# Key softmax on partitions, with bursts bound to places in TensorE's order, in an agent attention kernel with an MLP behind it

## The chip, the cores and the metric

The kernel runs on one core of one Trainium2 chip. The metric is the device time of one execution in microseconds. The core's engines are TensorE (PE in the profile; PEld is its weight load), VectorE (DVE), ScalarE (ACT), GpSimd (POOL) and SyncE (SP, which issues the DMAs). Each runs its own instructions in order.

## The reference

For four batches, 12480 tokens of 128 channels and 49 agents a batch:

```python
def sm(a, b):
    s = scale * (a @ b.transpose(0, 2, 1))
    s = s - s.max(-1, keepdims=True)
    e = np.exp(s)
    return e / (e.sum(-1, keepdims=True) + 1e-09)
a2k = sm(agents, k)
agent_v = a2k @ v
q2a = sm(q, agents)
x = (q2a @ agent_v).reshape(B * S, D)
h = x @ w_in            # 128 -> 2048
g = h - np.tanh(h)
return g @ w_out        # 2048 -> 128
```

The "key softmax" is `sm(agents, k) @ v`: each batch's 49 agents against all its keys.

## The kernel before, in words

Everything is built on a tile framework that places buffers, inserts semaphores and decides each engine's order by its own timeline; the program can add order edges, which wait for nothing by themselves but fix which instruction stands first in a queue (`hold`, L607; `issue_order`, L613).

The main loop (L791, in `fast`) runs over 100 blocks of 500 query columns, 8 steps a block; two blocks are a pair (16 positions, `pos`). A step is: m1 (L533), four matmuls of the queries' agent weights `pT` with the projected agent values in two parts (`awh`, `awl`), into a PSUM tile `h`; on ScalarE `y` = tanh (L548) and `z` = square (L550); on VectorE `g` = h*z (L553); on GpSimd `gh`, a rounded copy of g (L582); on VectorE `gl` = g - gh (L587); and m2 (L590), six matmuls (L600 to L602) that add to the block's output `acc`. m2 of a step is written two steps after its m1 (LAG1, LAG2). In every even block the last step is "plain": it has no gh and gl, and its m2 is L598. PSUM has three double banks for `h` and two banks, `misc`, for all else: the running `acc` holds one of them.

Beside the steps run jobs, written as generators: `start` takes the first stage of a job at the end of a step, and each later step takes one more stage, after its m1 and before its m2 (L808 to L814). Three kinds matter:

- `q_softmax` (L485) for the next pair, started at position QS = 3 from the second pair on. Its burst is 32 matmuls in 32-column tiles (L494): a quarter tile of q columns is stationary, the 49 agents move. Later stages reduce, copy (L502, L503), subtract on GpSimd (L505), take exp (L507), normalise and split.
- `q_transpose` (L520), which transposes its result (L525) and copies it to `pT` (L530), started at positions 13 and 2.
- The key softmax of the next batch, `phase1(b + 1)`: a list of 34 jobs, three to a pair, at positions KS = (4, 10, 15) for the first of them and VS = (5, 10, 13) for the rest: 13 score groups of 8 key tiles, the maximum, 13 value groups (`av`), the sum, and four projections.

In batches 1 to 3 a score group loads the agents, padded to 64 columns (`agz`), as the stationary operand and moves 128 keys: 8 matmuls into two halves of 64 partitions, so that agents lie on partitions and keys along the free axis (L279). ScalarE copies the result to `s` (L281), VectorE reduces each row to a maximum (L282). `max_in` (L284) joins the groups and the halves to one maximum for each agent, `mn`. A value group then has five stages: exp with that maximum as bias (L324, held behind the step's z); four transposes on TensorE, which bring keys back to partitions (L330); a ScalarE copy `ke` (L333); 8 matmuls of ke with 128 channels of v and a column of ones (L340); and an addition to `acc` in SBUF on VectorE (L352). Batch 0 is treated before the main loop with keys on partitions all the way: L300 and L311 bring its maximum to all partitions by a transpose and a ones matmul, L356 subtracts, L358 takes exp, L370 multiplies with v.

Of the kernel before, what the change touches and what calls it, by code (L numbers as in the profile page):

```python
# [12 lines left out]
F32 = mybir.dt.float32  # L13
# [4 lines left out]
ET = mybir.EngineType  # L18
# [47 lines left out]
QL = 0  # L66
QS = 3
T0 = 13
T1 = 2
KS = (4, 10, 15)  # L70
VS = (5, 10, 13)

# [25 lines left out]
class Build:  # L98
    def __init__(self, ctx, tc, aps):
        self.tc, self.nc = tc, tc.nc  # L100
        self.qT, self.kT, self.v, self.agT, self.wi, self.wo, self.outT = aps
        self.pool = lambda name, bufs=1, **kw: tc.tile_pool(name=name, bufs=bufs, **kw)
        self.const = ctx.enter_context(self.pool("const"))
        self.keep = ctx.enter_context(self.pool("keep"))
        self.small = ctx.enter_context(self.pool("small", 2))
        self.ph = ctx.enter_context(self.pool("ph", 3, space=PSUM))
        self.pmisc = ctx.enter_context(self.pool("pmisc", 2, space=PSUM))

    def begin(self, ctx, name):
# [8 lines left out]
    def constants(self):  # L118
        nc = self.nc
        c = self.const  # L120
        self.agz = c.tile([128, B, HALF], F32, tag="ag", name="ag")
        self.ag = self.agz[:, :, :A]
        nc.sync.dma_start(self.ag, self.agT.rearrange("b c a -> c b a"))
        nc.gpsimd.memset(self.agz[:, :, A:], 0.0)
        self.ident = c.tile([128, 128], F32, tag="ident", name="ident")
# [70 lines left out]
    def phase1(self, b):  # L196
# [36 lines left out]
        def scores(g):  # L233
            yield
            yield
            if g == 0:
                st["s"] = self.keep.tile([128, NG * 512], F32, tag="s", name="s", bufs=1)
                if b == 0:
                    st["mxp"] = self.work.tile([128, A, 2 * NG], F32, tag="mxp", name="mxp", bufs=1)
                else:  # L240
                    st["mxp"] = self.small.tile([128, NG], F32, tag="mxk", name="mxk")
                st["acc"] = self.small.tile([128, C + 1], F32, tag="acc", name="acc")
# [31 lines left out]
            ps = self.misc()  # L274
            w = n // 2 * 128
            for c in range(n // 2):
                for r in range(2):
                    to = ps[HALF * r : HALF * (r + 1), c * 128 : (c + 1) * 128]
                    nc.tensor.matmul(to, self.agz[:, b, :], kt[:, n // 2 * r + c, :], start=True, stop=True)  # L279
            yield  # L280
            nc.scalar.copy(st["s"][:, g * 512 : g * 512 + w], ps[:, :w])  # L281
            nc.vector.tensor_reduce(st["mxp"][:, g : g + 1], ps[:, :w], axis=AX.X, op=ALU.max)  # L282

        def max_in():  # L284
            yield
            yield
            if b:
                m = self.small.tile([128, 1], F32, tag="mk", name="mk")
                top = self.small.tile([128, 1], F32, tag="mt", name="mt")
                nc.vector.tensor_reduce(m, st["mxp"], axis=AX.X, op=ALU.max)  # L290
                nc.vector.tensor_copy(top[:HALF], m[HALF:])
                nc.vector.tensor_tensor(m[:HALF], m[:HALF], top[:HALF], ALU.max)
                nc.vector.tensor_copy(m[HALF:], m[:HALF])
                st["mb"] = self.small.tile([128, 1], F32, tag="mn", name="mn")
                nc.vector.tensor_scalar(st["mb"], m, -SCALE, None, ALU.mult)
                return
            m = self.small.tile([128, A], F32, tag="m", name="m")
            nc.vector.tensor_reduce(m, st["mxp"][:, :, 2 * EARLY :], axis=AX.X, op=ALU.max)
            ps = self.misc()
            nc.tensor.transpose(ps[:A, :128], m, self.ident)  # L300
# [16 lines left out]
        def av(g):  # L317
            vt = ahead("v", load_v, g, vb - 1) if b else None
            n = tiles(g)
            if b:  # L320
                w = n // 2 * 128
                e = st["s"][:, g * 512 : g * 512 + w]
                first = self.count()
                nc.scalar.activation(e, e, AF.Exp, bias=st["mb"], scale=SCALE)  # L324
                self.hold(first, self.act_at, (ET.Activation,))
                yield
                ps = self.misc()
                for c in range(n // 2):
                    sl = slice(c * 128, (c + 1) * 128)
                    nc.tensor.transpose(ps[:, sl], e[:, sl], self.ident)  # L330
                yield
                et = self.small.tile([128, 512], F32, tag="ke", name="ke")
                nc.scalar.copy(et[:, :w], ps[:, :w])  # L333
                yield
                ps = self.misc()
                for c in range(n // 2):
                    for r in range(2):
                        t = n // 2 * r + c
                        k = rows(g, t)
                        nc.tensor.matmul(  # L340
                            ps[HALF * r : HALF * (r + 1), : C + 1],
                            et[:k, c * 128 + HALF * r : c * 128 + HALF * (r + 1)],
                            vt[:k, t, : C + 1],
                            start=c == 0,
                            stop=c == n // 2 - 1,
                        )
                yield
                acc = st["acc"]
                if g == 0:
                    nc.vector.tensor_copy(acc, ps[:, : C + 1])  # L350
                else:
                    nc.vector.tensor_tensor(acc, acc, ps[:, : C + 1], ALU.add)  # L352
                return
            sv = st["s"][:, g * GT * A : (g * GT + n) * A].rearrange("p (t a) -> p t a", a=A)
            e3 = sv
            nc.vector.tensor_tensor(e3, sv, st["mb"][:, None, :].broadcast_to([128, n, A]), ALU.subtract)  # L356
            yield
            nc.scalar.activation(e3, e3, AF.Exp, scale=SCALE)  # L358
            yield
            vt = ahead("v", load_v, g, 1)  # L360
# [4 lines left out]
            flat = e3.rearrange("p t a -> p (t a)")  # L365
            for t in range(n):
# [31 lines left out]
        def sums():  # L398
            yield
            yield  # L400
            if b == 0:
# [15 lines left out]
                return  # L417
            acc = st["acc"]
            pt = self.misc()
            nc.tensor.matmul(pt[:, :A], acc[:, :C], self.sel, start=True, stop=True)  # L420
            rows_of = acc[:, C : C + 1].broadcast_to([128, 128])
            nc.tensor.matmul(pt[:, A:A2], rows_of, self.sel, start=True, stop=True)
            yield
# [61 lines left out]
    def q_softmax(self, halves, qt, res, TT=TT):  # L485
        nc = self.nc
        ps = self.misc()
        for t in range(GT):
            b, at, w = halves[t // BT]
            at += min(t % BT * TT, w - TT)  # L490
            for r in range(0, TT, QUART):
                m = min(QUART, TT - r)
                to = ps[r : r + m, t * A : (t + 1) * A]
                nc.tensor.matmul(to, qt[:, at + r : at + r + m], self.ag[:, b, :], start=True, stop=True)  # L494
        yield
        yield
# [83 lines left out]
    def high(self, g):  # L580
        gh = self.wtile("gh", NB["gh"])[:, : g.shape[1]].bitcast(F32R)
        self.nc.gpsimd.tensor_scalar(gh, g, 1.0, 0.0, ALU.mult, ALU.add)  # L582
        return gh

# [28 lines left out]
    def issue_order(self, engine, first):  # L613
        info = mybir.DependencyInfo(mybir.DependencyClass.NoSync, mybir.DependencyReason.DATA)
        last = None
        for i in list(self.nc.cur_bb.bb.instructions)[first:]:
            if i.engine == engine:
                if last is not None:
                    self.tc.add_manual_dep(i, last, info, reason="issue order")
                last = i.name  # L620

    def last_on(self, engine):
# [15 lines left out]
    def fast(self):  # L638
# [101 lines left out]
        run(rest0.pop(0))  # L740
        run(dec[0])
        live = []
        kq = []
# [18 lines left out]

        def foreground(n, i):
            h = self.m1(self.aw[blocks[n][0]], pT[n][0], i, width(n))
            while done:
                finish(done.pop(0))
            return h
# [13 lines left out]
        def out(keep):  # L781
            while len(r2) > keep:
                n, i, gh, gl = r2.pop(0)
                if i == 0:
                    acc[n] = self.misc()
                wf = self.wf[:, 2 * C * i :] if n == 0 else self.wo_f.rearrange("p c n -> p (c n)")
                self.m2(acc[n], i, gh, gl, wf)
                if i == HP - 1:
                    done.append(n)
# [56 lines left out]
        out(0)  # L846
        finish(done.pop(0))
        self.loads_first(early)

# [57 lines left out]
```

## Time and profile before

| | us |
|---|---|
| three runs | 2139.8, 2141.7, 2142.6 |
| median | 2141.74 |
| profiled execution | 2142.99 |
| its span | 2141.2 |
| granted TensorE clock | 0.996 |

The profile is of one execution. Busy times of TensorE overlap, since matmuls are pipelined: the start-to-start distance of two matmuls is what one of them takes of the engine. A matmul with f32 operands stands as two instructions ("x64" for 32 matmuls). In a row of groups, the numbers behind the bar are the busy time in us and the mean of one in ns, and behind the second bar the idle time just before. A row of the timeline gives start and duration in us; brackets hold idle time and what ended it.

### The profile page before, as it was taken

Reading aid. Unit: us, or ns where it says so; the run is one execution under the profiler, and the core shown is the slowest. Engines: PE = TensorE matmul, PEld = TensorE weight load, DVE = VectorE, ACT = ScalarE, POOL = GpSimd, SP = SyncE. Lnnn points to the kernel's source line nnn. Section 1 sums busy time; section 2 is a strip of 40 time slices with the busy share of each in tenths; the row PEclk is TensorE's granted clock in tenths of the full one; section 3 lists DMA queues with packets and bytes.
Section 4 is the critical chain, followed back from the end, with each engine's and each line's share of the span. In section 5 each row is a group of like instructions: output and inputs, shape, how many; then the busy total and the mean of one; then the engine's idle time right before and its main releaser. Section 6 shows DMA issues by size and latency. Waiting matters only on the chain.

```text
span 2141.2 us, 35133 instructions
## 1 busy us (share of the span) xinstructions
PE 2107.2 (98%) x13259; PEld 1658.2 (77%) x13259; DVE 1996.0 (93%) x2031; ACT 1820.5 (85%) x2136; POOL 1303.9 (61%) x858
## 2 busy tenths in 40 slices
PE   8999999999999999999999999999999999999998
PEld 7577778777777777777787777777777777778776
DVE  7899999889999998889999999988999999999998
ACT  3888888888888888888898888888888989899897
POOL 0366666556665556556576566655666767767666
PEclk9999999999999999999999999999999999999999
DMA  9312112110112111211001110111000000100000
GB/s 343 105 60 68 53 37 72 51 55 24 39 49 67 54 50 50 59 61 49 20 28 61 59 42 30 50 59 42 30 30 21 29 30 20 33 26 20 30 10 21
DMA packets 65345, 109.01 MB, mean 51 GB/s; under 512 B 3984, under 2 KB 44176, under 8 KB 65168
## 3 DMA queue, kind: packets, MB, share of 16 engines
q1 hardware_dynamic: 65168, 106.68, 15.2%
q8 instruction: 108, 1.77, 0.4%
q14 instruction: 69, 0.57, 0.1%
HBM read 81.10 MB, written 25.56 MB: 50 GB/s over the span
## 4 chain that ended last, share of the span: by engine, by line
PE 66%; DVE 18%; issue 6%; POOL 5%; ACT 4%; DMA 0%; POOLq 0%; SPq 0%; DVEq 0%; ACTq 0%
PE misc L602 12%; PE h L538 11%; PE misc L600 11%; PE h L539 11%; PE misc L601 10%; DVE g L553 9%; DVE gl L587 6%; POOL gh L582 4%; PE misc L598 3%; ACT y L548 2%; PE misc L340 2%; PE misc L494 2%; ACT z L550 1%; PE misc L279 1%; PE h L250 1%
## 5 line engine op out<-in xcount | busy, mean ns | idle before, releaser
L582 POOL TENSOR_SCALAR gh<-g 128x1000 fp32r<-128x1000 f32 (+1 forms) x743 | 1197.8, 1612 | 690.2 <-DVE g L553 387.5
L587 DVE TENSOR_TENSOR gl<-g,gh 128x1000 fp32r<-128x1000 f32 (+1 forms) x743 | 956.5, 1287 | 85.6 <-PE misc L602 42.9
L553 DVE TENSOR_TENSOR g<-h,z 128x1000 f32<-128x1000 f32 (+1 forms) x800 | 945.4, 1188 | 30.8 <-ACT z L550 28.8
L548 ACT ACTIVATE y<-h 128x1000 f32<-128x1000 f32 (+1 forms) x800 | 801.4, 1004 | 198.4 <-PE h L539 192.0
L550 ACT ACTIVATE z<-y 128x1000 f32<-128x1000 f32 (+1 forms) x800 | 823.1, 1041 | 29.2 <-DVE g L553 12.9
L538 PE MATMUL h<-pT,awh 98*128 98x500 f32 (+1 forms) x1600 | 662.5, 414 | 0.3
L539 PE MATMUL h<-pT,awl 98*128 98x500 f32 (+1 forms) x1600 | 622.0, 389 | 0.0
L602 PE MATMUL misc<-gl,wo_h 128*128 128x500 f32 (+1 forms) x1486 | 594.4, 400 | 8.2 <-DVE gl L587 7.9
L600 PE MATMUL misc<-gh,wo_l 128*128 128x500 f32 (+1 forms) x1486 | 581.7, 391 | 7.6 <-POOL gh L582 6.7
L601 PE MATMUL misc<-gh,wo_h 128*128 128x500 f32 (+1 forms) x1486 | 578.2, 389 | 0.0
L538 PEld LDWEIGHTS h<-pT,awh 98*128 98x128 f32 x1600 | 301.2, 188 | 79.8 <-issue 17.7
L539 PEld LDWEIGHTS h<-pT,awl 98*128 98x128 f32 x1600 | 303.3, 190 | 68.9 <-issue 14.5
L602 PEld LDWEIGHTS misc<-gl,wo_h 128*128 128x128 f32 x1486 | 279.0, 188 | 83.3 <-DVE gl L587 23.1
L600 PEld LDWEIGHTS misc<-gh,wo_l 128*128 128x128 f32 x1486 | 280.6, 189 | 75.3 <-POOL gh L582 21.6
L601 PEld LDWEIGHTS misc<-gh,wo_h 128*128 128x128 f32 x1486 | 279.7, 188 | 53.6
L505 POOL TENSOR_TENSOR qe<-qe,qm 126x392 f32<-126x392 f32 x50 | 46.9, 938 | 77.2 <-ACT qe L503 77.2
L517 POOL TENSOR_TENSOR pp<-qe,pp 126x392 fp32r<-126x392 f32 x50 | 55.6, 1113 | 59.6 <-ACT pp L515 59.5
L598 PE MATMUL misc<-g,wo_f 128*128 128x500 f32 (+1 forms) x196 | 90.0, 581 | 0.0
L758 ACT ACTIVATE o<-misc 128x500 f32<-128x500 f32 (+1 forms) x100 | 58.0, 580 | 16.2 <-PE misc L602 9.0
L530 ACT CAST pT<-misc 98x500 fp32r<-98x500 f32 (+1 forms) x100 | 56.7, 568 | 5.3 <-PE misc L525 4.4
L598 PEld LDWEIGHTS misc<-g,wo_f 128*128 128x128 f32 x196 | 36.9, 188 | 26.2 <-issue 22.5
L525 PEld LDWEIGHTS misc<-identr,pp 126*98 126x98 f32 x400 | 38.9, 127 | 18.4 <-POOL pp L517 6.5
(111 smaller groups left out, 853.7 us busy)
## 6 DMA issues: line engine op xcount, KB each, us to landing
kt<-kT SPq DMA_DIRECT2D x48, 512.0 KB, 3.7
qt<-qT SPq DMA_DIRECT2D x46, 500.0 KB, 3.5
outT<-o SPq DMA_DIRECT2D x46, 500.0 KB, 2.6
v<-v SPq DMA_DIRECT2D x36, 512.0 KB, 4.1
vt<-v SPq DMA_DIRECT2D x12, 512.0 KB, 5.8
raw<-w_in SPq DMA_DIRECT2D x4, 512.0 KB, 9.2
v<-w_out SPq DMA_DIRECT2D x4, 512.0 KB, 8.1
qt<-qT SPq DMA_DIRECT2D x4, 490.0 KB, 3.5
```

Of the source, the lines that this page charges most:

```text
L538: nc.tensor.matmul(h[:, c, :w], aw[0][:A2, sl], pT[:A2, :w], start=True, stop=False)
L539: nc.tensor.matmul(h[:, c, :w], aw[1][:A2, sl], pT[:A2, :w], start=False, stop=True)
L548: nc.scalar.activation(self.pair(y), h, AF.Tanh, scale=TSC)
L550: nc.scalar.activation(z, y, AF.Square)
L553: nc.vector.tensor_tensor(self.pair(g), h, self.pair(z), ALU.mult)
L582: self.nc.gpsimd.tensor_scalar(gh, g, 1.0, 0.0, ALU.mult, ALU.add)
L587: self.nc.vector.tensor_tensor(gl, g, gh.bitcast(F32), ALU.subtract)
L598: nc.tensor.matmul(acc[:, :w], wf[:, c * C : (c + 1) * C], gh[:, x], start=first, stop=last)
L600: nc.tensor.matmul(acc[:, :w], self.wo_l[:, f, :], gh[:, x], start=first, stop=False)
L601: nc.tensor.matmul(acc[:, :w], self.wo_h[:, f, :], gh[:, x], start=False, stop=False)
L602: nc.tensor.matmul(acc[:, :w], self.wo_h[:, f, :], gl[:, x], start=False, stop=last)
L758: nc.scalar.activation(o[:, at : at + w], acc[n][:, :w], AF.Copy, scale=GSC)
```

## The change

In batches 1 to 3 keys now lie on partitions. A score group is 32 matmuls in 32-column tiles, of the form of the query burst: a quarter key tile is stationary, the 49 agents move. Copy and reduction go over 392 elements instead of 512; partial maxima are kept per partition and agent, in a spare part of `s`, and `max_in` and `max_out` bring them to all partitions as for batch 0. A value group has four stages: the maximum is subtracted on GpSimd (held right behind the latest gh), exp is taken on ScalarE (held behind the latest z), e is the stationary operand of 8 matmuls (64 columns for even, 49 for odd tiles, in two column halves) with v moving, and VectorE adds 113 partitions to `acc`. The transposes and the copy `ke` are gone; so are the zero columns of `agz`.

In the main loop, each m1 and m2 group is noted in `stream`. The bursts of q, scores and values go through `burst`: their matmuls stand one behind the other, behind the last two noted groups, and the next six groups to be noted stand behind them. q_softmax starts one position sooner and has its burst a stage later, so that it stands after m1 of step 3 and not after m2; its copy and reduction come one step sooner. VS goes to (2, 7, 12).

```diff
-QS = 3
+QS = 2
-VS = (5, 10, 13)
+VS = (2, 7, 12)
...
 def scores(g):
-            w = n // 2 * 128
-            for c in range(n // 2):
-                for r in range(2):
-                    to = ps[HALF * r : HALF * (r + 1), c * 128 : (c + 1) * 128]
-                    nc.tensor.matmul(to, self.agz[:, b, :], kt[:, n // 2 * r + c, :], start=True, stop=True)
+            first = self.count()
+            for t in range(n):
+                for r in range(0, 128, QUART):
+                    to = ps[r : r + QUART, t * A : (t + 1) * A]
+                    nc.tensor.matmul(to, kt[:, t, r : r + QUART], self.ag[:, b, :], start=True, stop=True)
+            self.burst(first)
             yield
-            nc.scalar.copy(st["s"][:, g * 512 : g * 512 + w], ps[:, :w])
-            nc.vector.tensor_reduce(st["mxp"][:, g : g + 1], ps[:, :w], axis=AX.X, op=ALU.max)
+            nc.scalar.copy(st["s"][:, g * GT * A : (g * GT + n) * A], ps[:, : n * A])
+            nc.vector.tensor_reduce(st["mxp"][:, :, g], ps[:, : n * A].rearrange("p (t a) -> p a t", a=A), ...)
...
 def av(g):
+            first = self.count()
+            (nc.gpsimd if b else nc.vector).tensor_tensor(e3, sv, top, ALU.subtract)
+            if b:
+                self.hold(first, self.gh_at, (ET.Pool,))
+            yield
+            first = self.count()
             nc.scalar.activation(e3, e3, AF.Exp, scale=SCALE)
-            yield
+            if b:
+                self.hold(first, self.act_at, (ET.Activation,))
+            yield
+            if b:
+                ps = self.misc()
+                first = self.count()
+                for t in range(n):
+                    r = rows(g, t)
+                    odd = t % 2
+                    w = A if odd else HALF
+                    nc.tensor.matmul(
+                        ps[HALF * odd : HALF * odd + w, : C + 1],
+                        flat[:r, t * A : t * A + w],
+                        vt[:r, t, : C + 1],
+                        start=t < 2,
+                        stop=t >= n - 2,
+                    )
+                self.burst(first)
+                yield
...
-        jobs = [scores(g) for g in range(NG)] + [max_in(), max_out() if b == 0 else None, None]
+        jobs = [scores(g) for g in range(NG)] + [max_in(), max_out(), None]
...
 def q_softmax(self, halves, qt, res, TT=TT):
+        yield
         ps = self.misc()
+        first = self.count()
...
-        yield
+        self.burst(first)
         yield
...
+    def burst(self, first):
+        if self.stream is None:
+            return
+        names = [n for group in self.stream[-2:] for n in group]
+        for i in self.queued(first):
+            self.after(i, names)
+            names = [i.name]
+        self.gate = (len(self.stream), names)
+
+    def streamed(self, first):
+        at, names = self.gate
+        group = self.queued(first)
+        if len(self.stream) < at + 6:
+            for i in group:
+                self.after(i, names)
+        self.stream.append([i.name for i in group])
```

`queued` returns the TensorE instructions written since `first`; `after` adds order edges.

More of the change, by code (lines that the diff above doesn't have):

```diff
@@ L107, in __init__ @@
         self.pmisc = ctx.enter_context(self.pool("pmisc", 2, space=PSUM))
+        self.stream = None
     def begin(self, ctx, name):
@@ L240, in scores @@
                 else:
-                    st["mxp"] = self.small.tile([128, NG], F32, tag="mxk", name="mxk")
+                    st["mxp"] = st["s"][:, NG * GT * A :][:, : A * NG].rearrange("p (a g) -> p a g", g=NG)
                 st["acc"] = self.small.tile([128, C + 1], F32, tag="acc", name="acc")
@@ L286, in max_in @@
             yield
[L287 to L296, printed above, removed]
             m = self.small.tile([128, A], F32, tag="m", name="m")
-            nc.vector.tensor_reduce(m, st["mxp"][:, :, 2 * EARLY :], axis=AX.X, op=ALU.max)
+            part = st["mxp"] if b else st["mxp"][:, :, 2 * EARLY :]
+            nc.vector.tensor_reduce(m, part, axis=AX.X, op=ALU.max)
             ps = self.misc()
@@ L319, in av @@
             n = tiles(g)
[L320 to L325, printed above, removed]
-                yield
[L327 to L330, printed above, removed]
-                yield
[L332 to L353, printed above, removed]
@@ L620, in issue_order, with queued, after @@
                 last = i.name
+    def queued(self, first):
+        return [i for i in list(self.nc.cur_bb.bb.instructions)[first:] if i.engine == ET.PE]
+    def after(self, i, names):
+        info = mybir.DependencyInfo(mybir.DependencyClass.NoSync, mybir.DependencyReason.DATA)
+        for name in names:
+            self.tc.add_manual_dep(i, name, info, reason="order on TensorE")
+    def burst(self, first):
+        if self.stream is None:
+            return
+        names = [n for group in self.stream[-2:] for n in group]
[10 more added lines that the diff above has]
+        self.stream.append([i.name for i in group])
     def last_on(self, engine):
@@ L741, in fast @@
         run(dec[0])
+        self.stream, self.gate = [], (0, [])
         live = []
@@ L847, in fast @@
         finish(done.pop(0))
+        self.stream = None
         self.loads_first(early)
```

34 lines of the change are left out of this document (24 added, 10 removed).

## The prediction

> **What bounds the kernel now.** I read the page first, then the busy times of single stretches, then TensorE's timeline around the bursts that the change touches. A "pair" below is two blocks of 500 columns, sixteen steps of the main loop, so fifty pairs in all.
>
> ```profile
> span 2141.2 us, 35133 instructions
> PE 2107.2 (98%) x13259; PEld 1658.2 (77%) x13259; DVE 1996.0 (93%) x2031; ACT 1820.5 (85%) x2136; POOL 1303.9 (61%) x858
> PE 66%; DVE 18%; issue 6%; POOL 5%; ACT 4%; DMA 0%; POOLq 0%; SPq 0%; DVEq 0%; ACTq 0%
> ```
>
> TensorE is busy for 98% of the span and carries 66% of the chain that ended last, but VectorE is busy for 93% as well. A busy share of this size hides stages with different limits, so the next view takes three pairs apart: one in which three value groups (av jobs) are worked on, one with three score groups, and one late pair with no key work.
>
> ```profile
> core 0: us, PE busy (x) PEld busy (x) DVE busy (x) ACT busy (x) POOL busy (x), PEclk, DMA share, GB/s
> 357.20:400.50 43.30, 43.30 (x291) 34.46 (x290) 38.00 (x40) 37.98 (x45) 25.57 (x18) 1.00 0.20 61
> 650.90:693.20 42.30, 42.30 (x290) 32.76 (x288) 40.03 (x39) 35.70 (x42) 23.45 (x17) 1.00 0.20 63
> 1739.10:1778.20 39.10, 38.90 (x232) 30.89 (x231) 37.94 (x37) 34.73 (x40) 27.39 (x18) 1.00 0.08 27
> ```
>
> The reader is to see that an av pair takes 43.3 us and a score pair 42.3 us against 39.1 us without key work, and that in both TensorE never rests (43.30 of 43.30, 42.30 of 42.30) while VectorE, ScalarE and GpSimd have 2 us or more to spare. In those pairs only TensorE time counts. In the late pair VectorE has just 1.2 us left (37.94 of 39.10): there a delay to its chain shows. A batch's key work is 34 places in the job list (13 score groups, 3 for the maximum, 13 av groups, one sum, 4 projections), three to a pair, so over batches 1 to 3 there are about 13 score pairs, 13 av pairs, 8 mixed ones and 16 without.
>
> **TensorE's saving.** The bursts are costed from start to start, because the durations of pipelined matmuls overlap.
>
> ```profile
> 375.27 0.39 PE L600 MATMUL misc<-gh,wo_l 128*128 128x500 f32 x1
> 375.50 0.39 PE L601 MATMUL misc<-gh,wo_h 128*128 128x500 f32 x1
> 375.73 0.60 PE L330 MATMUL misc<-ident,s 128*128 128x128 f32 x4
> 376.08 0.47 PE L538 MATMUL h<-pT,awh 98*128 98x500 f32 x1
> 376.39 0.39 PE L539 MATMUL h<-pT,awl 98*128 98x500 f32 x1
> ...
> 381.40 0.49 PE L600 MATMUL misc<-gh,wo_l 128*128 128x500 f32 x1
> ...
> 681.00 0.39 PE L601 MATMUL misc<-gh,wo_h 128*128 128x500 f32 x1
> 681.32 1.09 PE L279 MATMUL misc<-kt,ag 128*64 128x128 f32 x16
> 682.35 0.49 PE L538 MATMUL h<-pT,awh 98*128 98x500 f32 x1
> 682.68 0.39 PE L539 MATMUL h<-pT,awl 98*128 98x500 f32 x1
> ...
> 1753.29 0.40 PE L601 MATMUL misc<-gh,wo_h 128*128 128x500 f32 x1
> 1753.62 0.90 PE L494 MATMUL misc<-ag,qt 128*32 128x49 f32 x64
> 1754.44 0.50 PE L602 MATMUL misc<-gl,wo_h 128*128 128x500 f32 x1
> 1754.78 0.39 PE L600 MATMUL misc<-gh,wo_l 128*128 128x500 f32 x1
> ```
>
> Stream matmuls follow each other every 0.23 us (375.27 to 375.50). The four transposes of an av group (L330) put 375.50 to 376.08 between two stream matmuls, 0.58 less 0.23, so 0.35 us, and the interval behind them is 0.31 instead of 0.23: 0.43 us in all. They vanish. The value burst itself (L340) keeps its number of passes, its 129 moving columns and its two column halves, with 49 instead of 64 stationary columns in the odd ones, and I leave it at 0.
>
> A score burst of today (L279, 16 passes) takes 1.35 less 0.23, and 0.10 behind it: 1.22 us. The new one has the form of the query burst (L494: 64 passes, 32 stationary columns, 49 moving), which costs 1.15 less 0.23, and 0.11: 1.03 us. That is 0.19 us less. Of the 39 groups 36 are full, and 36 x (0.43 + 0.19) is 22.3 us.
>
> The row for L494 has 64 passes in 0.82 us, 13 ns each, so passes into four column places do run beside each other. The Trainium skill, "TensorEngine Tiling (Array Packing)", Performance Considerations, speaks against this part: it says that a matmul has some 60 cycles of overhead and that no tiling factor should be taken from a dimension that is already small, and 49 columns lie below 60. By that page (an estimate from its figure, at the 2.4 GHz of "Trainium Kernel Development and Optimization", NeuronCore Architecture) the new burst would cost 64 x 25 ns / 4 = 0.40 us against some 0.43 for the old one, so no gain on scores and 7 us less in the sum; the measured rows, 0.82 and 1.03 from start to start, say that there is some, and they decide.
>
> New on TensorE is the maximum, which moves across partitions by a transpose and a ones matmul, as it does for batch 0 at the start:
>
> ```profile
> 32.14 0.29 PE misc L300
> 33.07 0.66 PE misc L311 x2
> ```
>
> That is 0.95 us for each of three batches, 3 us with what follows them. The net saving is 19 us.
>
> **The other engines.** These rows price what is removed and what comes.
>
> ```profile
> L324 ACT ACTIVATE s<-s,mn 128x512 f32<-128x512 f32 x36 | 25.5, 708 | 0.0
> L333 ACT COPY ke<-misc 128x512 f32<-128x512 f32 x36 | 21.1, 587 | 14.6 <-PE misc L330 14.6
> L281 ACT COPY s<-misc 128x512 f32<-128x512 f32 x36 | 21.1, 587 | 1.2 <-PE misc L279 1.0
> L503 ACT COPY qe<-misc 126x392 f32<-126x392 f32 x50 | 24.2, 483 | 17.7 <-DVE qm L502 17.7
> L507 ACT ACTIVATE qe<-qe 126x392 f32<-126x392 f32 x50 | 26.5, 529 | 0.0
> L505 POOL TENSOR_TENSOR qe<-qe,qm x50: 842/844/1785, 36.4 to 2070.7; 126x392 f32<-126x392 f32 x50
> ```
>
> ScalarE loses 0.71 + 0.59 + 0.59 and gets 0.48 + 0.53 us for each group, 0.87 less. VectorE keeps one reduction and one addition a group. GpSimd gets a subtraction of 128x392, 0.84 us like L505, 33 us in all on an engine that is 61% busy. None of this is worth time where TensorE has no rest; it is worth something only if a wait appears.
>
> **The new waits.** The change binds each q, k and e burst between two named groups of the stream: behind the last two groups written before it, ahead of the next six. TensorE works in order, so if the burst's input is late, m1 and m2 queue behind it. Today they fill such a wait. For scores the input is a key tile loaded two groups ahead, and a free misc bank, which I take as ready. For av it is a chain: GpSimd's gh of the step at which the job starts, then the subtraction, then exp, and two steps later the burst. Here is such a chain in an av pair:
>
> ```profile
> 381.96 0.39 PE L538 MATMUL h<-pT,awh 98*128 98x500 f32 x1
> 382.65 0.39 PE L539 MATMUL h<-pT,awl 98*128 98x500 f32 x1
> 382.88 0.40 PE L602 MATMUL misc<-gl,wo_h 128*128 128x500 f32 x1
> 383.08 1.01 ACT L548 ACTIVATE y<-h 128x1000 f32<-128x1000 f32 x1 [0.41 <-PE h L539]
> 384.12 1.04 ACT L550 ACTIVATE z<-y 128x1000 f32<-128x1000 f32 x1
> 385.19 1.20 DVE L553 TENSOR_TENSOR g<-h,z 128x1000 f32<-128x1000 f32 x1 [0.17 <-ACT z L550]
> 386.57 1.82 POOL L582 TENSOR_SCALAR gh<-g 128x1000 fp32r<-128x1000 f32 x1 [0.67 <-PE h L539]
> ```
>
> m1 ends at 383.04, gh at 388.39, 5.35 us later. With 0.84 and 0.53 and some 0.3 for three handovers (0.04 to 0.18 each in these rows), exp is done 7.0 us after m1, and up to one ScalarE operation (1.04) later if it finds the engine taken. Meanwhile TensorE has to run two more m1 groups (8 matmuls) and m2 up to one step back. At 381.40 to 382.88 it stood, at this m1, with two of six matmuls of the m2 four steps back done, so 4 + 18 of m2 are left: 30 matmuls of 0.227, 6.8 us. The binding itself keeps TensorE closer to the written order, where one group of four matmuls less is left: 26, 5.9 us. What else falls in the window decides:
>
> The job that starts at position 2 has the query burst (1.03) and a set of output transposes (about 0.3) ahead of it: 7.2 to 8.1 us against 7.0 to 8.0, a wait of 0 to 0.8, I take 0.2. At position 7 the step is the plain one, which has no gh; the subtraction goes behind the gh of step 6, ten matmuls or 2.3 us earlier, so 4.7 to 5.7 against 5.9: nothing. At position 12 only the transposes help: 6.2 to 7.1 against 7.0 to 8.0, a wait of 0 to 1.8, I take 0.4, near the end with the deeper order, since that is the one the trace shows. That is 0.6 us for an av pair, 8 us over 13, with bounds of 0 and 34. For the query and score bursts in all pairs I add 1 us, with the bounds in the rivals.
>
> **The sum.** 2143.0 us for the profiled execution (span 2141.2 and 1.8 around it), less 19, plus 9: 2133; the median of the runs before lies 1.2 lower, so 2132.
>
> **Rivals.** Everything ready: the bursts find their inputs, nothing waits, and the 19 us stay whole. For it speaks that the three positions are next to the query burst, on the plain step and next to the transposes; against it the narrow window at position 12. It gives 2123.
>
> The late exp: at positions 2 and 12 the chain has the length just worked out and TensorE the shorter window, with 0.8 and 1.8 us of idle TensorE in every av pair, 2.6 x 13 = 34 us, less 19 saved: 2157, slower than before. For it speaks that today's av burst has three steps between exp and its place and can be overtaken, and that the subtraction adds a handover on GpSimd. It decides from 0.5 us per av burst (19 us over 39). Against it: ScalarE is relieved by 0.87 us a group, and a TensorE that waits leaves the others less behind.
>
> The stream's own chain: a bound burst asks that the m2 three steps back be finished before the next m1 starts, four matmuls or 0.9 us sooner than today. In the 24 pairs without score or av jobs VectorE is 97% busy (37.94 of 39.10) and cannot deliver sooner; if TensorE waits 0.4 us behind the query burst in each, 10 us are gone and with 2142 the change is no change. What speaks for it is that late pair; against it that it is one place in sixteen steps.
>
> The tiling page's rule, as a mechanism here: passes below the fixed length gain nothing, the score part is 0 and 7 us are missing: 2139. The rows of L494 already show the price of this form, so it gets next to nothing.
>
> **Chances.** Forecast 0.38 (its own range 2126 to 2137), everything ready 0.10, cancelled 0.16, late exp 0.33, tiling rule 0.03. About 0.2%, 4.3 us, is what a measurement of this kernel can tell from no change. Faster is 0.48, from the first two; same 0.19, from the cancelled case and the tiling rule; slower 0.33. The range takes in the full saving with some 7 us below it, for gains that the start-to-start prices miss, and the late exp with 5 above: 2116 to 2162.
>
> **What would show it.** Right: L330 and L333 gone, score bursts of 64 passes with 0.82 us from their start to the next stream matmul, av pairs near 42.6 us and score pairs near 41.7, waits of TensorE for the exp line below 0.4 us on average, and the late pairs still at 39.1. Wrong: an average wait over 0.5 us ahead of the e matmuls; late pairs over 39.4; or VectorE, not TensorE, without rest in the av pairs, for which the subtraction beside gl would have to cost VectorE over 3 us a pair.

## The result

The changed kernel takes 2301.39 us (median of four runs, 2299.09 to 2302.46) against 2142.15 for the kernel before: a ratio of 1.0744, 95% interval 1.0726 to 1.0763. It is 159 us slower; 2132 was forecast, with a range up to 2162. Lines have moved: L532 and L533 are now m1, L595 to L597 m2, L488 the query burst, L278 the score burst, L337 the value burst with e stationary, L321 the subtraction on GpSimd, L326 exp.

The same page lines as before:

```profile
span 2300.6 us, 38536 instructions
PE 2144.3 (93%) x14885; PEld 1629.9 (71%) x14885; DVE 2034.3 (88%) x2028; ACT 1780.2 (77%) x2097; POOL 1297.0 (56%) x896
PE 54%; DVE 24%; ACT 9%; POOL 8%; issue 5%; DMA 0%; POOLq 0%; ACTq 0%; SPq 0%; DVEq 0%
```

TensorE fell from 98% to 93% busy and from 66% to 54% of the chain, and every other engine is busy for a smaller share of the longer span too: not a new bound, but waits. TensorE's idle time, the span less its busy time, rose from 34.0 to 156.3 us; these 122 us are most of the 159. The other 37 stand as busy time, at least in part because a matmul with another one right behind it counts for 0.23 us and one ahead of a stop for its whole 0.39. Three stretches show where. With pairs counted from 0 they are pairs 11 to 16 (projections and score groups of one batch), 17 to 22 (maximum and value groups) and 40 to 46 (no key work); first the kernel before, then the changed one; the columns are those of the prediction's table of pairs.

```profile
525.68:776.32 250.64, 249.06 (x1581) 194.53 (x1580) 239.97 (x234) 214.57 (x250) 151.25 (x103) 1.00 0.16 51
776.32:1033.60 257.28, 255.15 (x1636) 200.90 (x1635) 233.02 (x242) 222.68 (x263) 155.90 (x103) 1.00 0.16 50
1739.11:2012.34 273.23, 271.87 (x1611) 215.99 (x1610) 264.99 (x253) 242.70 (x274) 190.44 (x120) 1.00 0.08 27
```

```profile
571.53:833.07 261.54, 250.99 (x2171) 193.07 (x2169) 242.01 (x235) 211.10 (x249) 146.74 (x102) 1.00 0.16 49
833.07:1123.74 290.67, 263.13 (x1588) 193.87 (x1586) 245.22 (x240) 212.93 (x251) 163.44 (x116) 0.99 0.14 44
1883.14:2168.30 285.16, 275.13 (x1612) 215.30 (x1611) 260.51 (x253) 242.40 (x274) 183.47 (x120) 1.00 0.08 26
```

The score stretch lost 11 us, the value stretch 33 us, and even the seven late pairs lost 12 us, 1.7 each, although only their query burst was touched. In all three rows TensorE's own busy time is now well below the time of the stretch. What TensorE waited for, over the whole span (total in us, number of waits, longest in us):

```profile
PE misc L597 <- DVE gl L582: 67.8, 119, 1.5
PE misc L488 <- ACT pT L524: 27.6, 42, 0.9
PE misc L337 <- ACT s L326: 14.4, 14, 1.2
PE misc L595 <- POOL gh L576: 9.1, 19, 0.9
PE misc L337 <- ACT qe L497: 8.2, 12, 2.5
PE misc L519 <- ACT o L779: 7.8, 21, 0.7
```

Before, the first kind came to 7.9 us and the second and third did not occur. The second and the last belong together; this is TensorE in a late pair, and below it ScalarE:

```profile
1933.68 0.38 PE L597 MATMUL misc<-gl,wo_h 128*128 128x500 f32 x1
1934.45 0.48 PE L519 MATMUL misc<-identr,pp 126*98 126x126 f32 x4 [0.39 <-ACT o L779]
1935.59 0.90 PE L488 MATMUL misc<-ag,qt 128*32 128x49 f32 x64 [0.67 <-ACT pT L524]
1936.42 0.50 PE L595 MATMUL misc<-gh,wo_l 128*128 128x500 f32 x1
```

```profile
1933.83 0.56 ACT L779 ACTIVATE o<-misc 128x500 f32<-128x500 f32 x1
1934.96 0.57 ACT L524 CAST pT<-misc 98x500 fp32r<-98x500 f32 x1 [0.57 <-PE misc L519]
```

One misc bank goes from hand to hand: the output copy must leave it before the transposes can write, and pT must be copied out before the query burst can. The engines take turns, and TensorE, whose next stream groups may not pass the burst, stands for 0.39 and 0.67 us. The third kind, at the end of a value pair (TensorE, GpSimd, ScalarE):

```profile
1573.69 0.38 PE L597 MATMUL misc<-gl,wo_h 128*128 128x500 f32 x1
1575.28 1.09 PE L337 MATMUL misc<-v,s 128*64 128x129 f32 x16 [1.20 <-ACT s L326]
```

```profile
1571.93 1.82 POOL L576 TENSOR_SCALAR gh<-g 128x1000 fp32r<-128x1000 f32 x1 [0.39 <-PE misc L596]
1573.71 0.95 POOL L321 TENSOR_TENSOR s<-s,mb 128x392 f32<-128x392 f32 x1
```

```profile
1574.69 0.53 ACT L326 ACTIVATE s<-s 128x392 f32<-128x392 f32 x1 [0.53 <-POOL s L321]
```

gh ends at 1573.75, the subtraction at 1574.66, exp at 1575.22; TensorE was through with the groups ahead of the burst at about 1574 and waits for 1.2 us. The stop goes on behind it: no m1 starts between 1571 and 1577.7, and ScalarE gets no `h` for 3.72 us:

```profile
1578.94 1.93 ACT L542 ACTIVATE y<-h 128x1000 f32<-128x1000 f32 x2 [3.72 <-PE h L533]
```

### The profile page after: what moved, and what is told of

The parts are those of the page before. It is cut to its first block, busy times and chain, and to the rows that moved or that the text cites. A ratio compares the mean times of both kernels' runs of the same rounds, so it can differ in the third digit from the quotient of the medians.

```text
span 2300.6 us, 38536 instructions
## 1 busy us (share of the span) xinstructions
PE 2144.3 (93%) x14885; PEld 1629.9 (71%) x14885; DVE 2034.3 (88%) x2028; ACT 1780.2 (77%) x2097; POOL 1297.0 (56%) x896
## 4 chain that ended last, share of the span: by engine, by line
PE 54%; DVE 24%; ACT 9%; POOL 8%; issue 5%; DMA 0%; POOLq 0%; ACTq 0%; SPq 0%; DVEq 0%
DVE gl L582 11%; PE h L532 10%; DVE g L547 10%; PE h L533 9%; PE misc L597 9%; PE misc L595 8%; PE misc L596 8%; POOL gh L576 6%; PE misc L593 4%; ACT z L544 4%; ACT y L542 3%; POOL qe L499 1%; PE misc L337 1%; PE h L249 1%; PE misc L488 1%
## 5 line engine op out<-in xcount | busy, mean ns | idle before, releaser
L576 POOL TENSOR_SCALAR gh<-g 128x1000 fp32r<-128x1000 f32 (+1 forms) x743 | 1137.6, 1531 | 866.0 <-DVE g L547 758.2
L582 DVE TENSOR_TENSOR gl<-g,gh 128x1000 fp32r<-128x1000 f32 (+1 forms) x743 | 971.2, 1313 | 137.1 <-POOL gh L576 107.7
L542 ACT ACTIVATE y<-h 128x1000 f32<-128x1000 f32 (+1 forms) x800 | 791.4, 1002 | 167.4 <-PE h L533 163.1
L532 PE MATMUL h<-pT,awh 98*128 98x500 f32 (+1 forms) x1600 | 658.8, 412 | 2.9 <-DVE g L547 1.4
L597 PE MATMUL misc<-gl,wo_h 128*128 128x500 f32 (+1 forms) x1486 | 594.4, 403 | 67.8 <-DVE gl L582 67.8
L533 PE MATMUL h<-pT,awl 98*128 98x500 f32 (+1 forms) x1600 | 621.9, 389 | 0.0
L595 PE MATMUL misc<-gh,wo_l 128*128 128x500 f32 (+1 forms) x1486 | 595.6, 401 | 9.6 <-POOL gh L576 9.1
L597 PEld LDWEIGHTS misc<-gl,wo_h 128*128 128x128 f32 x1486 | 279.6, 188 | 176.2 <-DVE gl L582 122.8
L532 PEld LDWEIGHTS h<-pT,awh 98*128 98x128 f32 x1600 | 301.3, 188 | 104.9 <-issue 26.0
L533 PEld LDWEIGHTS h<-pT,awl 98*128 98x128 f32 x1600 | 303.0, 189 | 68.7 <-issue 13.7
L595 PEld LDWEIGHTS misc<-gh,wo_l 128*128 128x128 f32 x1486 | 280.5, 189 | 93.6 <-POOL gh L576 38.3
L499 POOL TENSOR_TENSOR qe<-qe,qm 126x392 f32<-126x392 f32 x50 | 70.9, 1418 | 52.9 <-ACT qe L497 52.9
L497 ACT COPY qe<-misc 126x392 f32<-126x392 f32 x50 | 24.3, 485 | 87.2 <-DVE qm L496 87.2
L511 POOL TENSOR_TENSOR pp<-qe,pp 126x392 fp32r<-126x392 f32 x50 | 49.2, 983 | 74.4 <-ACT pp L509 74.4
L488 PE MATMUL misc<-ag,qt 128*32 128x49 f32 (+1 forms) x3200 | 45.6, 210 | 27.9 <-ACT pT L524 27.6
```

The costliest lines, as they stand in the source:

```text
L499: nc.gpsimd.tensor_tensor(ev, ev, m[:TT, :, None].broadcast_to([TT, GT, A]), ALU.subtract)
L532: nc.tensor.matmul(h[:, c, :w], aw[0][:A2, sl], pT[:A2, :w], start=True, stop=False)
L533: nc.tensor.matmul(h[:, c, :w], aw[1][:A2, sl], pT[:A2, :w], start=False, stop=True)
L542: nc.scalar.activation(self.pair(y), h, AF.Tanh, scale=TSC)
L582: self.nc.vector.tensor_tensor(gl, g, gh.bitcast(F32), ALU.subtract)
L595: nc.tensor.matmul(acc[:, :w], self.wo_l[:, f, :], gh[:, x], start=first, stop=False)
```

## The experiments

The theory: all of the loss comes from binding the bursts, by way of inputs that are late while nothing may pass. Rivals: the new key softmax itself costs it; or the forced order of m1 and m2 does. "Value pairs" and "score pairs" in the expectations are means over pairs 7, 8, 19, 20, 32, 33 and over 3, 14, 15, 26, 27, 28. In kernels without binding, work moves over a pair's edge, so the stretches above, in us, are the better measure:

| kernel | whole | score | value | late |
|---|---|---|---|---|
| before | 2142.2 | 250.6 | 257.3 | 273.2 |
| changed | 2301.4 | 261.5 | 290.7 | 285.2 |
| e1 nothing bound | 2140.0 | 252.8 | 252.3 | 273.2 |
| e2 query burst free | 2260.6 | 254.2 | 291.4 | 273.1 |
| e3 transposes later | 2277.6 | 259.5 | 293.6 | 273.2 |
| e4 before, query burst bound | 2210.2 | 264.5 | 259.2 | 285.4 |
| e5 value bursts free | 2224.4 | 262.8 | 265.2 | 285.2 |
| e6 following groups may pass | 2141.5 | 253.4 | 253.8 | 273.1 |
| e7 one group looser | 2288.3 | 259.0 | 290.7 | 285.2 |
| e8 score bursts alone bound, looser | 2161.6 | 260.8 | 253.8 | 273.2 |
| e9 value burst a step later | 2209.8 | 262.1 | 259.5 | 285.2 |
| e10 nothing bound, score bursts whole | 2119.6 | 245.6 | 253.2 | 273.1 |
| e11 e9 and e3 | 2201.3 | 260.0 | 268.7 | 273.0 |
| e12 e11 and e7 | 2206.4 | 261.8 | 268.0 | 273.1 |

e1, e8 and e10 were timed four to ten times, with the kernel before beside them; each of the others is one execution. Thirteen executions of the kernel before lie between 2139.5 and 2143.1 us, so differences of a few us between single ones mean little. In e2 and e3 the granted clock over the span was 0.985 and 0.989, against 0.995 in the changed kernel; e2 shows what lies behind that.

**e1, nothing bound.**

```diff
-        self.stream, self.gate = [], (0, [])
+        self.stream, self.gate = None, (0, [])
```

> The changed kernel with no burst bound to a place: keys on partitions, the new positions and the subtraction on GpSimd stay. Theory 1, the binding costs the time (TensorE stands at bursts whose bank or whose exp is not ready): all of the 159 us go, and the 19 us of TensorE work saved show, 2120 to 2140 us, late pairs (no key work) back at 39.1 us. Rival, the key softmax itself costs it (the subtraction and the handover on GpSimd delay gh and gl): value pairs stay above 48 us, and the time above 2220 us.

2139.95 us, ratio 0.9992 (0.9982 to 1.0002): the loss is gone, so the key softmax with keys on partitions doesn't cost it. The saving, though, is not there: the value stretch is 5 us shorter than before, the score stretch 2 us longer. The timeline of TensorE shows one score burst in four pieces:

```profile
1195.62 0.39 PE L533 MATMUL h<-pT,awl 98*128 98x500 f32 x1
1195.94 0.46 PE L278 MATMUL misc<-ag,kt 128*32 128x49 f32 x22
1196.33 0.50 PE L595 MATMUL misc<-gh,wo_l 128*128 128x500 f32 x1
1196.67 0.39 PE L596 MATMUL misc<-gh,wo_h 128*128 128x500 f32 x1
...
1197.58 0.38 PE L533 MATMUL h<-pT,awl 98*128 98x500 f32 x1
1197.89 0.38 PE L278 MATMUL misc<-ag,kt 128*32 128x49 f32 x16
1198.20 0.49 PE L597 MATMUL misc<-gl,wo_h 128*128 128x500 f32 x1
...
1199.44 0.39 PE L596 MATMUL misc<-gh,wo_h 128*128 128x500 f32 x1
1199.76 0.46 PE L278 MATMUL misc<-ag,kt 128*32 128x49 f32 x22
1200.15 0.49 PE L597 MATMUL misc<-gl,wo_h 128*128 128x500 f32 x1
...
1200.94 0.39 PE L597 MATMUL misc<-gl,wo_h 128*128 128x500 f32 x1
1201.26 0.28 PE L278 MATMUL misc<-ag,kt 128*32 128x49 f32 x4
1201.47 0.50 PE L595 MATMUL misc<-gh,wo_l 128*128 128x500 f32 x1
```

Start to start, less 0.23 each, the pieces take 0.48, 0.39, 0.48 and 0.30, and every one has an interval of about 0.34 instead of 0.23 behind it: 2.1 us for a burst that, reckoned so, costs 1.02 whole (e10, below: 1.15 less 0.23, and 0.33 behind it). Only 11 of the 36 full bursts ran whole.

**e2, query burst free.** `self.burst(first)` is taken out of q_softmax; score and value bursts stay bound.

> The changed kernel with only the query burst free again, score and value bursts bound. Theory 1: the query burst waits in every pair for the misc bank, which goes from the output copy to the transposes, from them to the copy of pT, and only then to the burst. The late pairs, which have no other bound burst, fall from 40.7 to 39.1 us, and some 1.7 us in each of 46 pairs go: about 2222 us. Rival, the late pairs are slower for another reason than the bound query burst: they stay at 40.7 and the time near 2300.

The late pairs are back at 39.0, as expected, and the score stretch loses 7 of its 11 us. But the whole is 2260.6, 39 us above the expectation: in the value stretch nothing is won. There the bound value burst now waits for the bank that the free, later query burst holds:

```profile
PE misc L337 <- ACT qe L496: 44.0, 12, 3.7
```

Each of these 12 waits ends within 1.0 us of the start of a stretch of 3.4 or 6.8 us in which TensorE's clock is granted at one half (the 0.50 in the first row); the stream's matmuls then stand 0.42 us apart instead of 0.23:

```profile
934.60:941.40 6.80, 6.03 (x26) 4.92 (x27) 3.04 (x7) 1.54 (x3) 2.39 (x3) 0.50 0.27 78
938.28 0.62 PE L596 MATMUL misc<-gl,wo_h 128*128 128x500 f32 x1
938.70 0.62 PE L594 MATMUL misc<-gh,wo_l 128*128 128x500 f32 x1
```

Leaving out the first 60 and the last 30 us, e2 has 13 such stretches, in which half the clock adds up to 27 us; the changed kernel has three, with 5 us, and e1 and the kernel before have none. So up to 22 of the 39 us can be the clock, a second price of a long wait.

**e3, transposes later.**

```diff
-T1 = 2
+T1 = 5
```

> The changed kernel with the transposes of the pair's second block started at position 5 and not 2, so that they no longer stand ahead of the bound query burst in the misc bank; all bursts stay bound. Theory 1a, the bank chain: the late pairs fall to 39.1 to 39.5 us and the whole to 2215 to 2240. Theory 1b, the binding costs by the order that it forces on m1 and m2 and not by the bank: the late pairs stay above 40.3 and the time above 2285.

The late pairs are back at 39.0 with the query burst still bound, so there it was the bank and not the order of the stream. The whole fell by 24 us only, to a time between the two theories' ranges: the value stretch got 3 us longer, since its burst waits longer for the query's copy (29.0 us over the span, 8.2 in the changed kernel), and the half clock takes 8.5 us in it where it took 1.7.

**e4, the kernel before with the query burst bound.** QS = 2, the burst at step 3, `burst` and `streamed` as in the change; the key softmax untouched.

> The kernel before with the query burst alone treated as in the change (bound, started at position 2, burst at step 3); its key softmax with agents on partitions is untouched and its bursts free. Theory 1: some 1.7 us in every pair, late pairs at 40.7 us and the whole at 2205 to 2230 us. Rival, the key softmax itself costs the time: 2142 within 5 us.

2210.2, as expected: late pairs 40.8, and 14 us more in the score stretch. Binding costs the old key softmax as well.

**e5, value bursts free.** `self.burst(first)` is taken out of av.

> The changed kernel with only the value bursts (e stationary) free again; query and score bursts stay bound. Theory 2, binding the value bursts is what costs in the value pairs: they fall from 51.0 us to the 41.4 of the kernel without any binding plus the 1.7 of the bound query burst, about 43.1, and the whole to 2190 to 2210 us. Rival, in the value pairs too the query burst and its bank are the cause: they stay above 47 and the whole above 2245.

77 us of the 159 go, 25 of them in this one value stretch. The whole misses its range by 14 us, and value pairs stand at 44.4 for 43.1: the query burst costs more in them than the 1.7 of a late pair.

**e7, one group looser.**

```diff
-        names = [n for group in self.stream[-2:] for n in group]
+        names = [n for group in self.stream[-1:] + self.stream[-4:-3] for n in group]
```

> The changed kernel with all bursts bound, but one group looser: behind the last m1 and behind the m2 before the last one, so that the m2 of three steps back need not be finished first; the next six groups still stand behind the burst. Theory 2a, most of the loss comes from the forced order of m1 and m2 (VectorE's gl is not there yet): waits of TensorE for gl in the value pairs fall from 2.8 us to under 1, value pairs to 45 to 47, the whole to 2215 to 2245. Theory 2b, most comes from bursts whose own input is late and which nothing may pass: value pairs stay above 49, the whole above 2270.

The whole is 2288.3, and value pairs stay at 50.5 with the same waits for gl: theory 2b there, bursts whose own input is late. For the score bursts this run is no clean test: an m2 may now pass into a burst, and only 12 of the 36 full ones ran whole, where all 36 did in the changed kernel. The score stretch gains 2.5 us all the same.

**e9, value burst a step later.** One more `yield` between exp and the burst, all bursts bound.

> The changed kernel with one more step between exp and the value burst, all bursts bound. If late exp is what counts (the rival of the prediction that ended on the slower side): the 1.2 us of waiting for exp in a value pair go, with the waits that follow from them, value pairs at 47 us or less and the whole at 2250 or less. If it is the forced order of the stream: value pairs lose those 1.2 us at most, 49.5 to 51, the whole 2280 to 2300.

2209.8, the first case: the value stretch falls by 31 of its 33 us. TensorE's waits, first kinds:

```profile
PE misc L598 <- DVE gl L583: 39.7, 90, 1.5
PE misc L489 <- ACT pT L525: 18.6, 32, 0.9
```

The 14.4 us of waiting for exp and the 8.2 for the query's copy are gone, and 28 us of the waits for gl with them, so those came with the stops at the value bursts. How they come about is argued, not shown: while TensorE stands at the burst it runs no m1, and the chain from m1 to gl, 7 us long, starts late. In the trace of the changed kernel the waits for gl stand 8 to 16 us behind the bursts that waited for the query's copy, and none stands within 16 us behind a wait of 1.2 us for exp. Nor does e9 say which of the two waits costs how much: the burst asks for its bank a step later as well, so it takes both away.

**e8, score bursts alone bound, in the looser form.**

> The changed kernel with only the score bursts bound, in the looser form, query and value bursts free. Without any binding 25 of 36 score bursts are cut into two to four pieces and score pairs take 43.0 us against 42.1 before; a whole burst saves the 0.2 us that each further piece costs. If the pieces are the reason: score pairs at 41.5 to 42.2, the whole at 2122 to 2132 us, faster than both kernels. If a bound score burst costs by the order it forces, as query and value bursts do: score pairs above 43 and the whole 2140 or more.

2161.64, ratio 1.0096 (1.0079 to 1.0113): slower than the kernel before, and the hoped-for case did not come. Twelve score bursts now wait for the bank with the free query burst's result, 17.2 us:

```profile
PE misc L278 <- ACT qe L495: 17.2, 12, 2.0
```

Nor were the bursts whole: in the looser form 22 of the 36 full ones were cut. So this run does not answer whether the pieces cost the time; e10 does.

**e10, nothing bound, score bursts whole.** To e1, each matmul of a score burst gets an order edge to the one ahead of it, and from the second on they are written under `tc.high_priority()`.

> The changed kernel without any binding, but with each score burst kept whole: its matmuls stand one behind the other, and from the second on they go ahead of everything else in the program's order; where the burst begins is left free. Without binding 25 of 36 full score bursts were cut into two or more pieces, and score pairs took 43.0 us. If the pieces cost that time: score pairs at 41.3 to 42.0 us, value and late pairs as without binding (41.4 and 39.0), the whole at 2118 to 2130 us, which would be the saving of 19 us that the prediction worked out. If pieces are cheap and something else slows the score pairs: still 42.7 to 43.3, the whole 2136 to 2144.

2119.58, ratio 0.9899 (0.9882 to 0.9915), against 2141.04 of the kernel before: 1.0% faster than before, and the fastest here. The same stretches:

```profile
521.32:766.95 245.63, 245.11 (x2170) 194.74 (x2169) 236.70 (x235) 211.15 (x250) 152.41 (x102) 1.00 0.17 53
766.95:1020.15 253.20, 250.76 (x1587) 195.66 (x1586) 240.77 (x240) 212.76 (x250) 178.63 (x116) 1.00 0.17 51
1716.37:1989.49 273.12, 271.73 (x1611) 216.02 (x1610) 264.97 (x253) 242.65 (x274) 190.79 (x120) 1.00 0.08 27
```

And TensorE at one of its score bursts:

```profile
674.71 0.38 PE L600 MATMUL misc<-gl,wo_h 128*128 128x500 f32 x1
675.02 0.90 PE L281 MATMUL misc<-ag,kt 128*32 128x49 f32 x64
675.86 0.50 PE L598 MATMUL misc<-gh,wo_l 128*128 128x500 f32 x1
676.19 0.39 PE L599 MATMUL misc<-gh,wo_h 128*128 128x500 f32 x1
```

The burst has 0.84 us to the next start, and in this stretch TensorE is busy for 245.11 of 245.63 us again. The 21.5 us saved are close to the net 19 that the prediction worked out for TensorE.

**e11, both remedies, and e12, the looser binding as well.**

> The changed kernel, all bursts bound as in the change, with both remedies that worked one by one: one more step between exp and the value burst, and the transposes of the pair's second block started at position 5. If the two causes add up (bank chain at the query burst, late exp at the value burst): late pairs at 39.0, value pairs at 43.8 or less, score pairs near 44.5, the whole at 2145 to 2170 us. If moving the transposes brings the bank chain back at the value bursts: value pairs above 46 and the whole above 2180.

Late pairs 39.0 and score pairs 44.6 as expected, value pairs 44.5; but 2201.3, only 8 us less than e9. The two remedies don't add up: with the transposes later, value bursts wait again for the query's copy (11.2 us over the span; in the value stretch 3.7 us, and it is 9 us longer than in e9, from this wait alone and what follows it).

> All bursts bound, with one more step between exp and the value burst, the transposes started at position 5, and the looser binding (the m2 of three steps back may follow the burst). With the first two alone the score pairs still took 44.6 us, with 2.0 us of TensorE waiting for gl. If that is the forced order of m2: waits for gl in score pairs under 0.7 us, score pairs at 42 to 43.2 us, the whole at 2160 to 2182. If it is not: score pairs stay at 44.3 or more and the whole at 2195 or more.

Score pairs at 45.2 and the whole at 2206.4: the second case, loosening by one group doesn't remove what is left there. But as in e7 the looser form cuts bursts, here 23 of the 36 score bursts and 20 of the 50 query bursts. In the score stretch the waits for gl fell from 7.7 to 4.8 us, and TensorE's busy time rose from 250.7 to 254.9.

**e6, the following groups may pass.** The window of six following groups is set to none, the edges to the two groups ahead stay.

```diff
-        if len(self.stream) < at + 6:
+        if len(self.stream) < at + 0:
```

> The changed kernel with half of the binding: a burst stands behind the last two groups written before it, as in the change, but the next six groups need not stand behind the burst and may pass it. If the loss comes from TensorE being kept from other work while a burst or its bank is late, whichever input that is: value, score and late pairs as without any binding (41.4, 43.0, 39.0) within 0.5 us, the whole at 2135 to 2165 us. If it comes from the groups that have to be finished ahead of a burst: late pairs above 40.3, value pairs above 47, the whole above 2230.

2141.5, all stretches within 1.5 us of e1. So none of the 159 us is left without the half of the binding that keeps the following groups behind the burst; that half alone was not run. The score bursts stay whole here, yet the score stretch is no shorter than in e1: with the edges ahead, TensorE waits 20.2 us for gl instead of 7.8. It took whole bursts in a free place (e10) to get the saving.

## Why the prediction was wrong

The step that failed is the one under "The new waits": 0.6 us for an av pair, and "for the query and score bursts in all pairs I add 1 us". These 9 us stood for what measured 161 (2301.4 against 2140.0 without binding), or 182 against e10, which has the saving too. Two of the prediction's own signs of being wrong came: the value bursts waited for 0.58 us on average (14.4 and 8.2 us over 39 bursts), and the late pairs took 40.7 us.

- Query burst: the prediction named no input for it; "a free misc bank, which I take as ready" was said of the score bursts, and there it held, since TensorE has no wait at L278 in the changed kernel. At the query burst the bank is the last input; the transposes stand ahead of it there, and TensorE's wait is 1.1 us in a late pair, 1.7 with what follows (e2 and e3 take it away, e4 brings it into the old kernel). The rival for these pairs, the stream's own chain, had 0.4 us, from VectorE, which e3 rules out there; and e6, with the groups ahead of a burst still bound, loses nothing against e1.
- Value bursts: slower by way of late inputs at a bound burst was right, and so was the late exp of the second rival at position 12, with 0 to 1.8 us worked out and 1.2 measured. At position 2 it was not exp but the bank with the query's result that came late (0.3 us in ten waits, 2.5 in two), which no rival had. The price was far too low: 34 us for this rival, where e9 wins 92. Only the first wait was counted. The prediction saw that m1 queues behind the burst, but let it restart at no cost, whereas ScalarE then stands too and TensorE waits again, for gl.
- The saving on TensorE, 19 us, was nearly right in its sum, as e10 shows, with one condition that the prediction lacked: a burst must stay whole. In e1 the cut score bursts ate it. The parts fit less well: in the value stretch e10 gains 4.1 us, where 12 full groups at 0.43 less 1 for the maximum make 4.2, but in the score stretch 5.0, where 12 at 0.19 make 2.3, and pairs outside these stretches give some of it back (three times 9.1 would be 27 us, 21.5 came).
- The score burst, whole, takes 0.84 us from its start to the next stream matmul (e10), where the prediction's row had 0.82. The estimate of 0.40 by the Trainium skill, "TensorEngine Tiling (Array Packing)", Performance Considerations, is half of that. The page's warning is about the dimension that the factor is taken from, here a key tile of 128 columns, and not about the 49 moving columns, to which the prediction applied it; read in that way, 12 of the 19 us would have been left, and 21.5 came.
- ScalarE and GpSimd: without consequence wherever TensorE has no rest, as priced. The subtraction also makes VectorE's gl slower (last section), which the prediction put at nothing; in e1, which has it too, no time was lost by it.

What stays open: how the 92 us that e9 wins divide between the late exp and the late bank; and the score stretch of the fully bound kernel. There the bound query burst is what brings the loss: freeing it gives back 7.3 of the 8.7 us between the changed kernel and e1 (e2), and binding it alone in the old kernel adds 13.8 (e4). But with the bank free sooner the stretch still takes 259.5 and 260.0 us (e3, e11), with 7.4 and 7.7 us of waits for gl; by which input or order the query burst delays it there is not shown.

## What to carry to other kernels

An order edge that forbids work to pass makes an in-order engine wait for the burst's latest input, a free bank included; list the inputs and their chains before it is added. Price such a wait with what the standing engine itself would have started meanwhile, here four times the wait at the value burst (e9 wins 31 us in a value stretch with 8.1 us of such waits, and 92 us over the span with 22.6). Where a burst suffers from being cut, bind its pieces to each other and leave its place free.

## What the runs showed of the hardware

The same GpSimd subtraction (126x392, for the query softmax) has two durations: in the kernel before 45 of 50 took 0.85 us on average and five 1.70; in the changed kernel 31 took 1.76. Its row in the changed kernel, least, median and longest in ns:

```profile
L499 POOL TENSOR_TENSOR qe<-qe,qm x50: 842/1747/1783, 36.8 to 2223.6; 126x392 f32<-126x392 f32 x50
```

What decides is which of two instructions starts first, the subtraction or VectorE's gl, which reads two SBUF tiles. All 31 slow ones, and the five of the kernel before, began while gl was running; 18 in the kernel before that began while VectorE's g was running, with one input in PSUM, took 0.84 to 0.85 us. Where the subtraction began first it was quick and gl was slow: for the new subtraction this is so in 35 of 36 full groups, which took 0.94 to 0.98 us beside a gl of 1.83 to 1.95, while a gl with GpSimd at rest takes 1.20 (median). One pair of each kind:

```profile
670.13 1.20 DVE L582 TENSOR_TENSOR gl<-g,gh 128x1000 fp32r<-128x1000 f32 x1 [0.45 <-POOL gh L576]
670.28 1.75 POOL L499 TENSOR_TENSOR qe<-qe,qm 126x392 f32<-126x392 f32 x1 [0.19 <-ACT qe L497]
1573.71 0.95 POOL L321 TENSOR_TENSOR s<-s,mb 128x392 f32<-128x392 f32 x1
1573.78 1.94 DVE L582 TENSOR_TENSOR gl<-g,gh 128x1000 fp32r<-128x1000 f32 x1 [0.92 <-POOL gh L576]
```

The Trainium skill, "GPSIMD Engine Reference", Specifications, says that GpSimd shares its SBUF interfaces with VectorE and contends with VectorE instructions that have two SBUF inputs; the traces agree, with a factor of two for the subtraction that starts second. The prediction had taken the 0.84 us of the quick case for the new subtraction; its median is 0.955.
